# x sent ahead of the powers' row, two transfers moved to GpSimd's queue, guards earlier in a turn: a gated linear attention with a cosine MLP on one core

## The chip, the cores and the metric

The kernel runs on one core of a Trainium2 chip. The metric is device microseconds of that core. The kernel before takes 655.76 us in the median of 3 runs (654.2 to 656.69).

## The reference, cut to what matters

The inputs of the attention have batch 4, 8 heads, 768 steps and 48 channels per head; the MLP takes 3072 rows of 384 channels to 2048 and back. The weights of the MLP arrive as 64-bit floats.

```python
# attention: a gated linear recurrence with complex decay a, |a| capped at 0.999
for t in range(S):
    new_re = ar * S_re - ai * S_im
    new_im = ar * S_im + ai * S_re
    S_re, S_im = new_re + kv, new_im          # kv = outer(k[t], v[t])
    y[:, :, t] = einsum('bhd,bhde->bhe', q[:, :, t], S_re)
# MLP on x = y, with the heads side by side in a row of 384
h = x @ w_in
g = h * cos(h)
out = g @ w_out
```

## The kernel before

The 768 steps of each batch are cut into 6 chunks of 128 steps, and two chunks make a group: 24 chunks and 12 groups (n and g in the code run over them). Within a chunk the recurrence becomes matmuls: running products of the decays (their "powers" P and inverse powers Q) are multiplied into queries and keys, scores sc = k·q are masked into atm, and a state of 96x48 per head carries what came before. A group that begins a batch has no state in its first chunk; one that ends a batch makes no new state after its last chunk. So the groups come in three kinds that recur every three groups.

Groups 0 to 2 are laid out by hand. From group 2 on, a loop runs one turn for each n (line 1568 on), and in it lies work of several groups at once. weave() gives every piece of work a place between 0 and 1: the list chunks(n) spans 0.0 to 0.36, and its entries share that stretch evenly, so an entry's place depends on how many entries the list has. The entries are sorted by place, and a scheduler then settles the order on each engine with that as its priority. Each engine runs its own list in order.

In one turn n there are, by the names of the profile:

- **scores and attention of group n** (chunks): sc and its mask atm, sp (the state sums) and state, then yp, which ScalarE copies to yT. At its end f_x (line 1048) writes yT to DRAM as x, and f_xt (line 1057) reads it back, transposed, as xT.
- **the MLP of group n-1, second half** (products): matmuls into sum and op, and VectorE's ot<-op, which adds an op to a block of the output. out_dram<-ot stores it.
- **the powers of group n+1** (logs, prods): logarithms on ScalarE and VectorE; hi and lo, two halves of the log for exact sums; the matmuls lgs, with hi and lo as right sides; then exponentials into P (tile lg) and Q. When P is done, even_steps sends its last row to DRAM (row_out, line 835) and back, turned, as end (row_back, line 842).
- **phases and keys of group n+1**: phs, then ks and qs, turned by VectorE into tr, sent to DRAM as moved (line 933) and read back as kT (line 936) and qT (line 938).
- **the MLP of group n, first half** (first): 48 float32 matmuls into hp (shown as 96, since a float32 matmul is shown twice), which read xT; sines and products on ScalarE and VectorE.
- **guards** (from n = 4): GpSimd's queue fetches a piece of the 64-bit weights (raw<-in_moe...) once GpSimd has copied one element (after<-gate) to know that a gate is done; VectorE and ScalarE test its exponents. One buffer serves all guards in this part, so a second fetch waits for the first guard's test.

SyncE's queue carries all other transfers of a turn: the loads of re, im, k, q and v, row, x, end, xT, the outputs, moved, kT and qT. An instruction there that waits holds up those behind it. behind() and chain() only fix an order on a queue.

Of the kernel before, what the change touches and what calls it, by code (L numbers as in the profile page):

```python
# [487 lines left out]
def fast_path(ctx, tc, q, k, v, a_re, a_im, moe_w_in, moe_w_out, out, least, odd, wide,  # L488
# [7 lines left out]
    nc = tc.nc  # L496
    B, H, S, D = q.shape
# [45 lines left out]
    def behind(ins, other):  # L543
        tc.add_manual_dep(ins.ins, other.ins.name, mybir.DependencyInfo(
            mybir.DependencyClass.NoSync, mybir.DependencyReason.DATA))
# [21 lines left out]
    def load(g, names, i=None, put=nc.sync.dma_start):  # L567
        for name in names:
            ap = {"re": a_re, "im": a_im, "q": q, "k": k, "v": v}[name]
            if name not in X[g]:  # L570
                X[g][name] = ld.tile([C, G, H, D], F32, tag=name, name=name,
                                     bufs=2 if name == "v" else 1)
            b, c = divmod(g * G + (i or 0), NCH)
            one, n = i or 0, G if i is None else 1
            steps = ap[b].rearrange("h (c p) d -> p c h d", p=C)[:, ds(c, n)]
            tile_ = X[g][name][:, ds(one, n)]
            parts = [(0, C, 0)]
            if name in ("re", "im") and g >= PEG:

                parts = [(0, C - 16, 1), (C - 16, C - 1, 1)]  # L580
                put(out=tile_[C - 1:C], in_=steps[0:1])
            for i_ in range(n):
                for lo, hi, by in parts:
                    put(out=tile_[lo:hi, i_], in_=steps[lo + by:hi + by, i_])
# [227 lines left out]
    def even_steps(g, i, n):  # L812


        x = X[g]
        u = cut(x["mag"], i, n)
        P, Q = cut(x["P"], i, n), cut(x["Q"], i, n)
        ins = [vector.scalar_tensor_tensor(out=u, in0=Q, scalar=HUGE, in1=P,
                                           op0=ALU.min, op1=ALU.mult)]
        yield  # L820
        for t in P, Q:
            ins.append(vector.scalar_tensor_tensor(out=t, in0=u, scalar=3.0, in1=t,
                                                   op0=ALU.subtract, op1=ALU.mult))
            yield

        for one_, what in zip(ins, ("carried", "split")):
            if what in x and g > PEG:
                behind(one_, x[what])
        if g > 0:
            row_out(g, i, n, nc.sync)  # L830
            row_back(g, i, n, nc.sync)

    def row_out(g, i, n, queue):
        P = cut(X[g]["P"], i, n)
        queue.dma_start(out=X[g]["row"][ds(i * DM, n * DM)],
                        in_=P[C - 1:C].rearrange("o x -> (o x)"))

    def row_back(g, i, n, queue):
        row = X[g]["row"][ds(i * DM, n * DM)]
        end = X[g]["end"][:, ds(i * H, n * H)]  # L840
        for a in range(2):
            queue.dma_start(out=end[ds(a * D, D)], in_=row.rearrange("(x d) -> d x", d=D))

    def p_even(g, i, n):
        for _ in even_steps(g, i, n):
# [75 lines left out]
    def f_transpose(g, i, n, name):  # L921


        if i == 0:
            X[g][name] = ft.tile([D2, G * H, Q4, 32] if name == "kT" else [D2, Q4, G * H, 32], F32,
                                 tag=name, name=name, bufs=1)
        tr = ft.tile([C, NB, n * H, 32], F32, tag="tr", name="tr")
        turn = vector.transpose(out=tr, in_=X[g][name[0] + "s"][:, ds(i * H, n * H)].rearrange(
            "p x a d -> p x (a d)").rearrange("p x (r b) -> p b x r", b=NB))
        if name == "qT" and "gated" in X[g - 1]:  # L930
            behind(turn, X[g - 1]["gated"])
        moved = rows_d.tile([Q4, D2, n * H, 32], F32, tag="moved", name="moved", bufs=3)
        nc.sync.dma_start(out=moved.rearrange("q (r b) x j -> (q r) b x j", b=NB), in_=tr)
        if name == "kT":
            for q4 in range(Q4):
                nc.sync.dma_start(out=X[g][name][:, ds(i * H, n * H), q4], in_=moved[q4])
        else:
            nc.sync.dma_start(out=X[g][name][:, :, ds(i * H, n * H)],
                              in_=moved.rearrange("q c x j -> c q x j"))

    def f_turn(g, i, name, hh):

# [109 lines left out]
    def f_xt(g, i=0, n=G):  # L1052

        if i == 0:
            X[g]["xT"] = msb.tile([C, ND, G, C], F32, tag="xT", name="xT")
        moved = X[g]["moved"].rearrange("p s d g t -> (p s d) g t").rearrange("(c r) g t -> r c g t", r=C)
        put = nc.sync.dma_start(out=X[g]["xT"][:, :, ds(i, n)], in_=moved[:, :, ds(i, n)])
        behind(put, late["x"])
        late["x"] = put

    def mm1_sums(g, jp, i=None):

# [97 lines left out]
    def seventh(g, p, part):  # L1160


        x, name = X[g], SEVEN[p]
        if p == 0 and part == 0:
            x["sum"] = pm.tile([C, E2], F32, tag="acc", name="sum", bufs=1)
            x["ot"] = [msb.tile([C, DM], F32, tag="ot", name="ot") for _ in range(G)]

        alone = g == NG - 1 and p == 6
        summed = p in (0, 3, 5, 6) and not alone
        if not summed and part == 0:  # L1170
            x["op"] = pm.tile([C, E2], F32, tag="m", name="op", bufs=2)
        ps = x["sum"] if summed else x["op"]
        for j in range(part * HJ // 2, (part + 1) * HJ // 2):
            matmul(ps, lhsT=left(g, name, j), rhs=right[name][:, j],
                   start=(j == 0 and (p == 0 or not summed)),
                   stop=(j == HJ - 1), skip_group_check=summed)
        if part == 0:
            return
        c11, c12, c21, c22 = (x["ot"][i][:, ts(half, E2)] for i in range(2) for half in range(2))
        if g == NG - 1:  # L1180
            c12 = rest
        if p in (0, 3, 5) or p == 6 and not alone:
            late["scalar"] = scalar.mul(out={0: c11, 3: c21, 5: c22, 6: c12}[p], in_=ps, mul=scale)
        if g == NG - 1 and p == 5:
            scalar.mul(out=c12, in_=ps, mul=scale)
        for part_ in {1: [c11], 2: [c21], 4: [c21, c22], 6: [c12] * alone}.get(p, []):
            added = vector.scalar_tensor_tensor(out=part_, in0=ps, scalar=scale,
                                                in1=part_, op0=ALU.mult, op1=ALU.add)
            if alone:
                behind(added, late["read DVE"])  # L1190
            late["vector"] = added
        row = g * G * C
        if g == NG - 1 and p == 1:
            behind(nc.sync.dma_start(out=out[ds(row, C), 0:E2], in_=c11), late["line"])
        elif p == 4:
            put = nc.sync.dma_start(out=out[ds(row + C, C), :], in_=x["ot"][1])
            if g == NG - 1:
                behind(put, late["read SP"])
        elif p == 6 and alone:
            late["store"] = lambda: nc.scalar.dma_start(out=out[ds(row, C), E2:DM], in_=c12)  # L1200
        elif p == 6:
            nc.sync.dma_start(out=out[ds(row, C), :], in_=x["ot"][0])
# [57 lines left out]
    def chunks(g):  # L1260
        for n in range(g * G, g * G + G):
            for hh in range(2):
                yield lambda n=n, hh=hh: f_scores(n, hh)
            yield lambda n=n: f_state(n)
            yield lambda n=n: f_out(n)
        yield lambda: (f_x(g), f_xt(g))
        if g + 2 < NG:
            yield lambda: load(g + 2, ("k", "q", "v"))

    def first(g):  # L1270
        order = range(NJ // 2) if g < PLAIN else (0, 4, 1, 5, 2, 6, 3, 7)
# [2 lines left out]
    def second(g, i):  # L1274
        return [lambda j0=j0: mm2(g, i, j0, 4) for j0 in range(0, NJ, 4)] if g < PLAIN else []
# [292 lines left out]
    for n in range(2, NG):  # L1568
        weave((mixes(n - 1, 2, 4), 0.0, 0.12), (logs(n + 1), 0.0, 0.02), (chunks(n), 0.0, 0.36),
              (upper[2:] if n == 2 else [], 0.0, 0.2), (products(n - 1, 0, 2 + (n < NG - 1)), 0.0, 0.36),  # L1570
              (prods(n + 1), 0.25, 0.27), (second(n - 1, 1), 0.36, 0.5),
              (products(n - 1, 2 + (n < NG - 1), 7), 0.4, 0.56),
              (phases(n + 1), *((0.472, 0.476) if n == PLAIN else (0.516, 0.524))),
              (keys(n + 1), *((0.5, 0.62) if n == PLAIN else (0.53, 0.64))),
              (last_quarter() if n == PLAIN else [], 0.9, 1.0), (first(n), 0.56, 1.0),
              (mixes(n, 0, 2), 0.9, 1.0), (guarded(n - 1, per) if n > 3 else [], 0.1, 0.9))
    checked = verdict(late, temp)

    def judged():
# [98 lines left out]
```

## Time and profile before

The profiled execution took 653.01 us; its span is 651.2 us, and 1.8 us lie around it.

| what | value |
|---|---|
| median of 3 runs | 655.76 us (654.2 to 656.69) |
| profiled execution, span | 653.01 us, 651.2 us |
| TensorE busy (matmuls), weight loads | 98%, 89% of the span |
| VectorE, ScalarE, GpSimd busy | 76%, 60%, 5% |
| clock granted to TensorE | 1.00 |
| one turn of the loop | 50.2 to 51.7 us, the last 48.1 us |
| SyncE's queue: share of 16 DMA engines | 45.3% |
| GpSimd's queue: share of 16 DMA engines | 11.7% |

A turn is measured here from the first hp matmul of one group to that of the next. The busy share of a matmul row says only that something was in the array; whether the array was delayed is seen from the waits and from the distance between groups of matmuls.

### The profile page before, as it was taken

Reading aid. Unit: us, or ns where it says so; the run is one execution under the profiler, and the core shown is the slowest. Engines: PE = TensorE matmul, PEld = TensorE weight load, DVE = VectorE, ACT = ScalarE, POOL = GpSimd, SP = SyncE. Lnnn points to the kernel's source line nnn. Section 1 sums busy time; section 2 is a strip of 40 time slices with the busy share of each in tenths; the row PEclk is TensorE's granted clock in tenths of the full one; section 3 lists DMA queues with packets and bytes.
Section 4 is the critical chain, followed back from the end, with each engine's and each line's share of the span. In section 5 each row is a group of like instructions: output and inputs, shape, how many; then the busy total and the mean of one; then the engine's idle time right before and its main releaser. Section 6 shows DMA issues by size and latency. Waiting matters only on the chain.

```text
span 651.2 us, 10758 instructions
## 1 busy us (share of the span) xinstructions
PE 641.0 (98%) x4075; PEld 576.4 (89%) x4075; DVE 492.0 (76%) x799; ACT 392.8 (60%) x726; POOL 30.9 (5%) x53
## 2 busy tenths in 40 slices
PE   8999999999999999999999999999999999999997
PEld 6888877777999999899899899899899999999996
DVE  6999989888687688786787787876877878862251
ACT  7898687284583593494494485485576476433330
POOL 4010200000000000010010010000000000000000
PEclk9999999999999999999999999999999999999999
DMA  9968755727627656747738737836836843363001
GB/s 249 244 179 203 225 164 123 170 62 182 146 49 182 158 146 148 194 110 167 209 82 191 204 85 167 205 96 151 226 105 146 219 123 98 112 134 120 25 1 31
DMA packets 232920, 94.90 MB, mean 146 GB/s; under 512 B 208701, under 2 KB 221246, under 8 KB 232858
## 3 DMA queue, kind: packets, MB, share of 16 engines
q1 hardware_dynamic: 225320, 68.51, 45.3%
q0 software_dynamic: 5824, 25.50, 11.7%
q8 instruction: 34, 0.56, 0.4%
q10 hardware_dynamic: 1714, 0.11, 0.2%
q14 instruction: 28, 0.23, 0.1%
HBM read 69.28 MB, written 24.81 MB: 144 GB/s over the span
## 4 chain that ended last, share of the span: by engine, by line
PE 92%; ACT 4%; DVE 3%; DMA 0%; issue 0%; SPq 0%; DVEq 0%
PE hp L687 38%; PE op L687 18%; PE sum L687 16%; PE sc L687 6%; PE yp L687 6%; PE sp L687 4%; PE phs L687 2%; PE lgs L687 1%; ACT tan L707 1%; PE yr L687 1%; PE tp L948 1%; ACT rs L707 1%; ACT lg L707 1%; ACT L703 1%; DVE mag L676 1%; DVE atm L676 1%
## 5 line engine op out<-in xcount | busy, mean ns | idle before, releaser
L687 PE MATMUL hp<-xT,w_in 128*128 128x256 f32 (+1 forms) x1176 | 252.5, 375 | 0.0
L687 PEld LDWEIGHTS hp<-xT,w_in 128*128 128x128 f32 x1176 | 219.6, 190 | 30.2 <-issue 0.2
L707 ACT ACTIVATE gate<-hp,half_pi_b 128x512 f32<-128x512 f32 x96 | 66.0, 687 | 118.5 <-PE hp L687 118.5
L687 PE MATMUL op<-w_out,gate 128*128 128x192 f32 (+1 forms) x448 | 100.7, 374 | 0.0
L676 DVE TENSOR_TENSOR gate<-hp,gate 128x512 f32<-128x512 f32 x96 | 65.7, 684 | 45.8 <-ACT junk L676 45.7
L687 PEld LDWEIGHTS op<-w_out,gate 128*128 128x128 f32 x448 | 75.9, 190 | 16.9 <-issue 2.0
L676 ACT ACTIVATE junk<-hp 128x512 bf16<-128x512 f32 x96 | 56.7, 591 | 0.0
L687 PE MATMUL sum<-t_s,s 128*128 128x192 f32 x320 | 56.3, 329 | 0.0
L687 PEld LDWEIGHTS sum<-t_s,s 128*128 128x128 f32 x320 | 52.1, 190 | 1.5 <-issue 1.5
L676 DVE TENSOR_TENSOR atm<-sc,causal 128x512 f32<-128x512 f32 x48 | 32.9, 689 | 23.4 <-PE sc L687 23.4
L687 PEld LDWEIGHTS sc<-qT,kT 96*128 96x128 f32 x384 | 47.4, 192 | 2.3 <-issue 0.6
L687 PE MATMUL sc<-qT,kT 96*128 96x128 f32 x384 | 49.0, 276 | 0.2 <-ACT qT L676 0.2
L676 ACT ACTIVATE ot<-sum 128x192 f32<-128x192 f32 x39 | 12.6, 322 | 53.7 <-PE sum L687 53.4
L676 DVE SCALAR_TENSOR_TENSOR ot<-op,ot 128x192 f32<-128x192 f32 x40 | 13.3, 354 | 38.0 <-PE op L687 36.4
L687 PE MATMUL yp<-atm,v 128*48 128x128 f32 x352 | 33.6, 277 | 0.9 <-ACT Q L707 0.6
L703 ACT ACT_TABLE_LOAD x24 | 30.8, 1283 | 1.2 <-PEq L1662 0.7
L676 ACT COPY yT<-yp 48x512 f32<-48x512 f32 x44 | 25.3, 574 | 7.4 <-PE yp L687 7.0
L687 PE MATMUL yp<-qT,state 96*48 96x128 f32 x304 | 29.7, 272 | 0.0
L687 PE MATMUL sum<-w_out,gate 128*128 128x192 f32 x160 | 29.7, 329 | 0.0
L687 PE MATMUL sp<-v,ks 128*96 128x48 f32 x320 | 29.7, 245 | 0.0
L687 PEld LDWEIGHTS sp<-v,ks 128*96 128x96 f32 x320 | 29.6, 165 | 0.0
L676 ACT CAST tan<-phs 128x384 int32<-128x384 f32 x24 | 11.4, 480 | 29.4 <-PE phs L687 29.4
(147 smaller groups left out, 987.4 us busy)
## 6 DMA issues: line engine op xcount, KB each, us to landing
moved<-tr SPq DMA_DIRECT2D x20, 768.0 KB
raw<-in_moe_w_in_dram POOLq DMA_DIRECT2D x16, 768.0 KB, 5.1
raw<-in_moe_w_out_dram POOLq DMA_DIRECT2D x16, 768.0 KB, 4.6
kT<-moved SPq DMA_DIRECT2D x40, 192.0 KB
qT<-moved SPq DMA_DIRECT2D x10, 768.0 KB
k<-in_k_dram SPq DMA_DIRECT2D x24, 192.0 KB
q<-in_q_dram SPq DMA_DIRECT2D x24, 192.0 KB
v<-in_v_dram SPq DMA_DIRECT2D x24, 192.0 KB
```

The costliest lines, as they stand in the source:

```text
L676: ins = getattr(self.engine, op)(**kw)
L687: chain(nc.tensor.matmul(out, **kw), "tensor")
L703: chain(nc.scalar.preload_act_table_set(table))
L707: chain(nc.scalar.activation(func=func, **kw))
L948: chain(nc.tensor.transpose(ps[:, h], X[g][name[0] + "s"][:, x0 + h].rearrange("p a d -> p (a d)"), ident), "tensor")
```

## The change

- On SyncE's queue, for groups after the second, P's row is no longer sent when P is done, but in a step of its own, ends(n+1), woven in at 0.36 to 0.37, after x (and ordered behind it). end follows.
- The load of k, q and v two groups ahead, which was the last entry of chunks(n), goes into ends(n+1), each DMA ordered behind end. chunks(n) has 9 entries instead of 10.
- xT, from group 2 on, and qT, from group 3 on, are issued from GpSimd's queue, where they stand in one fixed order with the guards' fetches.
- One store of the output (p == 4) is ordered behind end and the loads.
- The guards are woven in at 0.0 to 0.38 of a turn, not 0.1 to 0.9.

```diff
@@ even_steps
-        if g > 0:
-            row_out(g, i, n, nc.sync)
-            row_back(g, i, n, nc.sync)
+        if 0 < g <= PLAIN:
+            ends(g)
+
+    def after_ends(**kw):
+        put = nc.sync.dma_start(**kw)
+        behind(put, late["ends"])
+        late["ends"] = put
+
+    def ends(g):
+        put = row_out(g, 0, G, nc.sync)
+        if g > PLAIN:
+            behind(put, late["x"])
+        row_back(g, 0, G, nc.sync)
+        if PLAIN < g < NG - 1:
+            load(g + 1, ("k", "q", "v"), put=after_ends)
@@ row_back
-            queue.dma_start(out=end[ds(a * D, D)], in_=row.rearrange("(x d) -> d x", d=D))
+            late["ends"] = queue.dma_start(out=end[ds(a * D, D)], in_=row.rearrange("(x d) -> d x", d=D))
@@ f_transpose
-            nc.sync.dma_start(out=X[g][name][:, :, ds(i * H, n * H)],
-                              in_=moved.rearrange("q c x j -> c q x j"))
+            queue = nc.sync if g <= PLAIN else nc.gpsimd
+            put = queue.dma_start(out=X[g][name][:, :, ds(i * H, n * H)],
+                                  in_=moved.rearrange("q c x j -> c q x j"))
+            if g > PLAIN:
+                chain(put, "gpsimd")
@@ f_xt
-        put = nc.sync.dma_start(out=X[g]["xT"][:, :, ds(i, n)], in_=moved[:, :, ds(i, n)])
-        behind(put, late["x"])
-        late["x"] = put
+        queue = nc.sync if g < PLAIN else nc.gpsimd
+        put = queue.dma_start(out=X[g]["xT"][:, :, ds(i, n)], in_=moved[:, :, ds(i, n)])
+        if g >= PLAIN:
+            chain(put, "gpsimd")
@@ seventh
-            if g == NG - 1:
-                behind(put, late["read SP"])
+            behind(put, late["read SP"] if g == NG - 1 else late["ends"])
@@ chunks
-        if g + 2 < NG:
-            yield lambda: load(g + 2, ("k", "q", "v"))
@@ the loop of turns
-              (prods(n + 1), 0.25, 0.27), (second(n - 1, 1), 0.36, 0.5),
+              (prods(n + 1), 0.25, 0.27),
+              ([lambda: ends(n + 1)] if n + 1 < NG else [], 0.36, 0.37), (second(n - 1, 1), 0.36, 0.5),
...
-              (mixes(n, 0, 2), 0.9, 1.0), (guarded(n - 1, per) if n > 3 else [], 0.1, 0.9))
+              (mixes(n, 0, 2), 0.9, 1.0), (guarded(n - 1, per) if n > 3 else [], 0.0, 0.38))
```

More of the change, by code (lines that the diff above doesn't have):

```diff
@@ L828, in even_steps @@
                 behind(one_, x[what])
-        if g > 0:
-            row_out(g, i, n, nc.sync)
-            row_back(g, i, n, nc.sync)
+        if 0 < g <= PLAIN:
[11 more added lines that the diff above has]
+            load(g + 1, ("k", "q", "v"), put=after_ends)
     def row_out(g, i, n, queue):
         P = cut(X[g]["P"], i, n)
-        queue.dma_start(out=X[g]["row"][ds(i * DM, n * DM)],
-                        in_=P[C - 1:C].rearrange("o x -> (o x)"))
+        return queue.dma_start(out=X[g]["row"][ds(i * DM, n * DM)],
+                               in_=P[C - 1:C].rearrange("o x -> (o x)"))
     def row_back(g, i, n, queue):
```

## The prediction, written before the changed kernel was run

> **What bounds the kernel now.** I read the page first, then TensorE's waits, then turns as windows, then the chain of waits and the timeline inside a turn. The page gives 98% for TensorE's matmuls; since matmuls overlap, I don't take that as proof. TensorE's waits are the proof (columns: waiting group, releaser, us in total, times, longest):
>
> ```profile
> PE busy L687 <- DVE one_b L557: 1.5, 1, 1.5
> PE phs L687 <- ACT tan L707: 1.4, 2, 0.8
> PE yp L687 <- ACT Q L707: 0.6, 1, 0.6
> PE tp L948 <- DVE ks L676: 0.6, 2, 0.4
> ...
> PE sc L687 <- ACT qT L676: 0.2, 1, 0.2
> ```
>
> Seven rows sum to 5.1 us, and none is a wait for a transfer (the last row is a copy by ScalarE at the start, at 23.5 us); the change hurries transfers. Turns, as windows from hp to hp (start:end, us, then busy us of each engine):
>
> ```profile
> 204.16:255.37 51.21, 51.21 (x349) 47.89 (x347) 40.10 (x65) 31.81 (x60) 1.86 (x3) 1.00 0.62 156
> 255.37:305.61 50.24, 50.09 (x332) 46.46 (x332) 38.65 (x62) 31.80 (x60) 1.85 (x3) 1.00 0.63 155
> 305.61:355.93 50.32, 50.32 (x332) 47.00 (x331) 39.76 (x64) 31.79 (x60) 1.85 (x3) 1.00 0.65 162
> ...
> 507.69:559.38 51.69, 51.54 (x349) 47.93 (x347) 40.40 (x68) 31.77 (x60) 1.78 (x3) 1.00 0.48 129
> ```
>
> The first three are the three kinds of turn, all dense with matmuls. The fourth is of the first's kind (349 matmuls) and 51.69 - 51.21 = 0.48 us longer. It is turn n = 10, where the list of chunks had no load left to append (there is no group 12), so it had 9 entries instead of 10. That is the order the change gives to all turns n = 3 to 10. The kernel before thus holds one specimen of the new order, and the chain of waits shows its price (start, us, what):
>
> ```profile
> 537.82 0.91 PE sc L687 x8
> 538.72 0.02 issue
> 538.75 0.69 DVE atm L676
> 539.44 0.86 DVE mag L676
> 540.30 0.88 DVE lo L676
> 541.18 0.04 issue
> 541.22 0.79 PE lgs L687 x3
> 542.02 1.32 PE sp L687 x16
> ```
>
> The chain leaves TensorE for VectorE: lgs waits for lo. In the other turns that make a state, sp stands ahead of lgs and fills this time.
>
> **What the Trainium skill says.** "TensorE: Matmul & The Clock Gate", its first table: the array may pull weight loads ahead, while VectorE and ScalarE keep strict order. The trace agrees: lgs' weight load sat 0.40 us for lo, and sp behind it didn't overtake. "DMA: Bandwidth & Descriptors", Specifications, puts the first byte at about 1 us for GpSimd's queue and 0.6 us for SyncE's. The packets' records of this trace have 0.9 us (a guard issued at 289.42, first packet 290.33) and 0.6 us (xT issued at 301.52, first packet 302.13). "SBUF — State Buffer", two separate sides, warns that VectorE's two-port modes keep GpSimd from writing descriptors; the guards' fetches here, issued beside VectorE's work, show no such delay, but none sits beside the keys' VectorE work as qT will.
>
> **The change part by part.**
>
> *x first, xT on GpSimd.* In turn n = 5 yT was ready at 294.93 (copy 294.35 + 0.58), but x issued at 298.33, behind P's row at 297.98 (lg done 296.97 + 0.95). xT issued at 301.52; its last packet ended at 304.31. x's own landing was noticed 1.0 us after its last packet (300.54), so xT was usable by about 305.3, and hp's loads began at 305.45. Over the eight turns from hp at 153.84 to 507.69 the last packet ends 1.3 to 2.4 us ahead of hp, a real slack of 0.3 to 1.4 us. The change starts x up to 3.4 us sooner, less 0.3 us for the slower queue. In the profiled execution this gains nothing, as hp never waited. What is late next is matmul work itself.
>
> *qT on GpSimd.* It no longer queues behind the four kT (314.25 to 319.04), so it can start some 1.7 us sooner. Its last packet came 1.1 to 2.5 us before sc. Only in turn n = 10 could it have cost anything: sc took 0.96 instead of 0.89, and hp 20.79 instead of 20.72. Gain 0 to 0.1; I take 0. If descriptors starve, qT has about 1 + 1.7 us in hand.
>
> *Queues passed.* On GpSimd's queue the order in a turn becomes after, guard, guard, xT, qT. The second fetch waited 9.55 us for the first guard's test and left at 289.42, before x can land (about 298), so xT isn't held: 0. On SyncE's queue row and end still go when P is ready (297.9); p_end needed end only at 308.67. The loads keep their place: 0. Of end's packets and the k loads, which compete with xT, fewer now overlap it.
>
> *Guards sooner.* Both tests already run in the first 45% of a turn in the trace (VectorE's raw at 284.86 and 294.75 in the turn 255.37 to 305.61). They hardly move: 0.
>
> *The reordering on TensorE, from the shorter list.* The entries of chunks move from 0.036 to 0.040 apart. That puts the second state sum from place 0.234 to 0.26, behind lgs (prods start at 0.25); it also parts the second chunk's sc by an op (sc op sc instead of sc sc op). In the built program's order turns n = 3 to 10 read: sc, op, sc, lgs, sp, half a sum, yp, half a sum. The matmuls' number is unchanged. Price by kind:
>
> - n = 5, 8 (no second state): before, lgs already waits: 1.35 us from lgs to the next group against 0.87 elsewhere. By groups before: .89+1.30+.90+1.32+1.46+1.90+1.40+1.79+1.16+1.35+1.90+2.71 = 18.08. After, with the specimen's durations: .89+1.30+.90+1.30+1.41+1.90+1.40+.89+1.31+.81+1.20+1.46+1.90+1.41 = 18.08. Change 0.
> - n = 4, 7: become the specimen: 2 x 0.48 = 0.96, of which 0.07 was in hp, so 2 x 0.41 = 0.8.
> - n = 10: 0.
> - n = 3, 6, 9 (no state at first): VectorE's order there also changes, to atm, ot, mag, lo. ot needs the second op complete. From op at 333.21 (n = 6): first state sums 0.09 longer and ahead of yp, so op starts about 333.13, + 1.40 + 0.89 + 1.31 = op complete at 336.73, sc to 337.54, where lgs is due. ot starts 0.2 later than op's end, 336.95; then 0.27 to mag, 0.87 to lo (both step sizes are those of neighbouring starts in the timeline), lo at 338.1 and done 0.95 later: 339.05. hi, on ScalarE, moves too: an ot and a copy of yT now precede it, 336.35 to about 337.0, done 337.85, so mag and lo can't be sooner than 337.2 and 338.1 either. lgs' low half would have been loaded at 337.73; it stalls 1.35 us. Before there was no stall there (0.87). 3 x 1.35 = 4.05.
>
> ```profile
> 336.35 0.83 ACT L728 ACTIVATE hi<-lg 128x768 fp32r<-128x768 f32 x1
> 337.20 0.95 DVE L676 TENSOR_TENSOR mag<-mag,tan 128x768 f32<-128x768 f32 x1
> 338.07 0.95 DVE L676 SCALAR_TENSOR_TENSOR lo<-lg,hi 128x768 fp32r<-128x768 f32 x1
> 339.81 0.35 DVE L676 SCALAR_TENSOR_TENSOR ot<-op,ot 128x192 f32<-128x192 f32 x1
> ```
>
> Before, ot came after lo, as the last row shows, and sp hid what was left.
>
> Sum in the profiled execution: 0.8 + 4.05 = +4.9 us, 653.0 to 657.9. Bounds: if ot and hi cost no more than in the specimen, 5 x 0.41 = +2.1; if the later yp (1.5 us, for half a sum stands before it) and a ScalarE order with yT behind hi make x late as well, up to 0.5 a turn, +4 more.
>
> **From the profiled execution to the median.** The three runs took 1.2 to 3.7 us more than the profiled one, 2.75 at the median. The trace doesn't show where. Slack of 0.3 us for xT makes late transfers a fair suspect, and those the change would cure: between 0 and all 2.75. I take half. 655.76 + 4.9 - 1.3 = 659.4.
>
> **Rivals.**
>
> - *Only the specimen's price* (+2.1): lgs stalls 0.4 in five turns, since ot turns out not to gate lo. For it: one measured specimen. Against: VectorE's order, and hi. 655.76 + 2.1 - 1.3 = 656.6.
> - *Not slower: the runs' surplus is xT late at hp.* One mechanism: at the eight hp starts with 0.3 to 1.4 us of slack, ordinary scatter of the DMAs costs 2.75 / 8 = 0.34 us each, and x's early start removes it all. It decides once the surplus removed exceeds the stalls added; with the rival above's +2.1 it gives 655.76 - 2.75 + 2.1 = 655.1, with no stalls 653.0. For it: slack under jitter. Against: no wait for xT in any turn traced.
> - *GpSimd's queue holds xT or qT.* A guard's test delayed behind other ScalarE work keeps the second fetch, and so xT, back. ScalarE's test would have to slip by over 8 us; then each microsecond beyond costs 8 turns x 1 us: 665 and more.
>
> **How the numbers follow.** Forecast 0.5, specimen's price 0.22, not slower 0.18, GpSimd's queue 0.10. The time is 659.4. Its own spread is 658.0 (all the surplus gone) to 660.7 (none). The range takes in the specimen's case and the upper half of the third: 654.5 to 661.5. About 0.5% (3.3 us) is what a measurement tells from no change: slower means over 659.0, faster under 652.5. Faster lies below even a stall-free loop, 653.0: 0.06. Slower: 0.6 of the forecast's 0.5 and the queue's 0.10, plus a little of the others: 0.46. The rest, 0.48, is within 0.5%.
>
> **What would show it.** After should show lgs waiting for lo in eight turns, over 1 us in n = 3, 6, 9 and 0.4 in the others; sp right behind lgs; x issued ahead of row; xT and qT on GpSimd's queue with 2 us or more in hand. No lgs waits, or hp beginning late, would prove me wrong; so would turns of 50.3 us throughout.

## The result, and the profile after

The changed kernel takes 660.63 us in the median of 6 runs (659.78 to 661.47), beside 655.07 us for the kernel before on the same chip (6 runs, 653.68 to 656.69). The ratio is 1.0083, with a 95% interval of 1.0068 to 1.0098: slower by 5.6 us. Its profiled execution took 660.9 us, with a span of 659.0 us; the one before had 653.01 and 651.2.

TensorE's waits after the change (columns as before: waiting group, releaser, us in total, times, longest). Groups that also waited before are left out, and two rows of 0.2 us:

```profile
PE lgs L687 <- DVE lo L676: 3.0, 5, 0.9
...
PE hp L687 <- DMA xT<-x: 0.9, 1, 0.9
PE sc L687 <- DMA kT<-moved: 0.8, 1, 0.8
```

The first row is the stall that the prediction describes. The other two are waits for transfers, which the profile before did not have at all. The page still gives 98% busy to TensorE's matmuls, as before: the busy share hides all three.

What the change was meant to do for xT, it does: for groups 2 to 9, xT's last count (the last of the 16 marks by which a transfer reports that it has landed) comes 1.6 to 3.9 us ahead of hp, beside 0.4 to 1.5 us before. As no hp waited for it before, that gains nothing in these two profiles.

Turns of the changed kernel as windows (start:end, us, then busy us of PE, PEld, DVE, ACT, POOL; clock, DMA share, GB/s). They are the turns n = 3, 4, 5, 6, 10 and 11:

```profile
154.14:206.86 52.72, 50.98 (x332) 47.15 (x331) 38.96 (x62) 29.88 (x56) 1.45 (x2) 1.00 0.63 138
206.86:258.42 51.56, 51.41 (x347) 48.05 (x347) 40.27 (x65) 31.85 (x60) 3.32 (x5) 1.00 0.61 153
258.42:308.60 50.18, 50.03 (x333) 46.68 (x331) 38.66 (x62) 31.76 (x60) 3.12 (x5) 1.00 0.64 157
308.60:360.25 51.65, 50.75 (x331) 47.25 (x331) 39.84 (x64) 31.87 (x60) 3.31 (x5) 1.00 0.62 154
...
514.04:565.73 51.69, 51.54 (x349) 47.96 (x347) 40.31 (x68) 31.86 (x60) 3.24 (x5) 1.00 0.44 121
565.73:614.83 49.10, 48.24 (x322) 44.71 (x321) 25.17 (x44) 16.41 (x38) 3.24 (x5) 1.00 0.43 121
```

Turn n = 6 (308.60) now takes 51.65 us where its kind took 50.32, with no more matmul work in it: PE is busy for 50.75 us and idle for 0.90. Turn n = 10, the specimen, is unchanged to the hundredth. Turns n = 3 and n = 11 are longer than their kinds for another reason, which comes below.

The chain of waits inside turn n = 6 (start, us, what):

```profile
337.70 0.89 PE sc L687 x8
338.59 1.32 PE op L687 x8
339.91 0.02 issue
339.93 0.36 DVE ot L676
340.29 0.86 DVE mag L676
341.15 0.88 DVE lo L676
342.03 0.04 issue
342.08 0.80 PE lgs L687 x3
342.88 1.32 PE sp L687 x16
```

The chain leaves TensorE when op ends, goes through three operations of VectorE, ot, mag and lo, and comes back with lgs; sp, which filled this stretch before, stands behind lgs and cannot overtake it.

All turns, in us from hp to hp, with the difference that the prediction gave (its 1.35, 0.41 and 0) beside the one measured between the two profiled executions:

| turn n | 3 | 4 | 5 | 6 | 7 | 8 | 9 | 10 | 11 | sum |
|---|---|---|---|---|---|---|---|---|---|---|
| before | 50.32 | 51.21 | 50.24 | 50.32 | 51.21 | 50.23 | 50.32 | 51.69 | 48.07 | 453.61 |
| after | 52.72 | 51.56 | 50.18 | 51.65 | 51.57 | 50.58 | 51.64 | 51.69 | 49.10 | 460.69 |
| difference | 2.40 | 0.35 | -0.06 | 1.33 | 0.36 | 0.35 | 1.32 | 0 | 1.03 | 7.08 |
| predicted | 1.35 | 0.41 | 0 | 1.35 | 0.41 | 0 | 1.35 | 0 | 0 | 4.87 |

In n = 3, 1.01 us of the 2.40 lies in the distance from hp to sc (21.73 for 20.72): kT is late. In n = 8, 0.33 of the 0.35 lies there too, and kT's last count came at 432.63, just ahead of sc at 432.87. In n = 11, 1.03 us stands in front of the last hp: xT is late. Without these 2.37 us, 4.71 us are left for the reordering.

Two theories follow. The first is the prediction's: the reordering on TensorE, which comes from the shorter list of chunks, costs the time, and the moved transfers gain or lose little. Its rival: the new places of the transfers (x, xT, qT, row, end, loads) cost it, by holding or crowding one another.

### The profile page after: what moved, and what is told of

It is laid out like the page before. It is cut to its first block, busy times and chain, and to the rows that moved or that the text cites. A ratio compares the mean times of both kernels' runs of the same rounds, so it can differ in the third digit from the quotient of the medians.

```text
span 659.0 us, 10778 instructions
## 1 busy us (share of the span) xinstructions
PE 643.3 (98%) x4075; PEld 577.6 (88%) x4075; DVE 492.4 (75%) x799; ACT 393.2 (60%) x726; POOL 44.9 (7%) x72
## 4 chain that ended last, share of the span: by engine, by line
PE 85%; DMA 4%; ACT 4%; DVE 4%; issue 1%; SPq 1%; DVEq 0%; POOLq 0%
PE hp L687 35%; PE op L687 16%; PE sum L687 15%; PE yp L687 6%; PE sc L687 5%; PE sp L687 4%; PE phs L687 2%; DMA x<-yT 1%; PE lgs L687 1%; DVE mag L676 1%; DMA kT<-moved 1%; DVE lo L676 1%; ACT tan L707 1%; PE yr L687 1%; PE tp L963 1%; DMA moved<-tr 1%
## 5 line engine op out<-in xcount | busy, mean ns | idle before, releaser
L687 PE MATMUL sum<-t_s,s 128*128 128x192 f32 x320 | 57.8, 330 | 0.0
```

Source lines behind the costliest of these rows:

```text
L687: chain(nc.tensor.matmul(out, **kw), "tensor")
```

## The experiments

### The order alone, and the transfers alone

**e2_nine** takes the kernel before, with all its queues, and only makes the list of chunks shorter by moving the load out of it into a part of its own.

```diff
@@ chunks (in the kernel before)
-        if g + 2 < NG:
-            yield lambda: load(g + 2, ("k", "q", "v"))
@@ the loop of turns
+              ([lambda: load(n + 2, ("k", "q", "v"))] if n + 2 < NG else [], 0.35, 0.355),
```

> The kernel before with nothing but the list of chunks shortened to nine entries (the load of k, q, v becomes a part of its own at 0.35); all queues as before. Reordering theory: 655.1 + 4.6 = 659.7 us, ratio 1.007, turns of 51.65, 51.55 and 50.2 us. Queue theory: 655, ratio 1.000, since no transfer moved.

It took 660.51 us (658.64 to 663.3) beside 655.31, ratio 1.0072 (1.0043 to 1.01). TensorE's waits in it:

```profile
PE lgs L687 <- DVE lo L676: 2.8, 4, 0.9
PE hp L687 <- DMA xT<-x: 2.4, 1, 2.4
...
PE sc L687 <- DMA qT<-moved: 0.9, 1, 0.9
```

The lgs row of the changed kernel is there, without any change of queue, and TensorE works through its groups of matmuls in the same order as after the change, from the first to the last. Its turns n = 4 to 7 take 51.56, 50.16, 51.64 and 51.56 us, the same as after the change within 0.02. So the shorter list alone gives a slowdown of the size of the whole: 5.2 us, by the interval 2.8 to 6.6. The late xT here lies ahead of the first of these turns, the late qT in n = 10; how much of them is in the ordinary runs is not known.

**e1_ten** goes the other way: the changed kernel with an empty tenth entry in the list, so that places return to 0.036 apart.

```diff
@@ chunks (in the changed kernel)
         yield lambda: (f_x(g), f_xt(g))
+        if g + 2 < NG:
+            yield lambda: None
```

> The changed kernel with an empty tenth entry in the list of chunks, which brings TensorE's order of before back; all queue moves stay. If the reordering is what costs (4.6 us of the changed kernel's turns by its trace), about 656.0 us, ratio to before 1.001 to 1.002, and lgs stands behind sp without a wait. If the transfers on GpSimd's queue are what costs, it stays near 660, ratio 1.007. If both, the rest above 655 is kT or xT late by about 1 to 2 us.

It took 667.39 us (663.55 to 670.23), ratio 1.0172 (1.0135 to 1.0208): a miss. The order on TensorE was that of before, and lgs no longer waited for lo but in the turns where it did before (0.87 us from lgs to the next group in n = 3, 6 and 9). But other waits had come:

```profile
PE sc L687 <- DMA kT<-moved: 5.8, 5, 2.0
PE hp L687 <- DVE gate L676: 2.6, 6, 0.5
```

GpSimd's queue shows why (timeline; start, us, engine, line, operation, idle before and its releaser):

```profile
249.50 0.76 POOL L1073 DMA_DIRECT2D xT<-x  x1 [19.28 <-DMA x<-yT]
250.25 0.74 POOL L629 DMA_DIRECT2D raw<-in_moe_w_in_dram  x1
```

The entry had moved xT to place 0.306, ahead of the second fetch at 0.317. On a queue with one fixed order the second fetch, which the changed kernel issues in this turn at 240.91, more than 9 us ahead of xT, now had to wait for x to land, and went out beside the loads of k, q and v. The issue of the two moved that follow took 5.35 us (3.15 in the changed kernel), and kT came late. In one stretch of 3.4 us, after its longest wait for kT, the clock granted to TensorE was 0.5 besides. So this kernel differs in two things, and its time alone tells nothing of the order.

**f1_order_of_before** mends that: the empty entry, and the guards at 0.0 to 0.36 so that both stay ahead of xT. The order on TensorE, VectorE and ScalarE is then that of the kernel before, but for a guard's test in two turns and one ot; the queues of SyncE and GpSimd are those of the changed kernel. From e1_ten it differs in the guards' place alone.

```diff
@@ chunks (in the changed kernel)
+        if g + 2 < NG:
+            yield lambda: None
@@ the loop of turns
-              ... (guarded(n - 1, per) if n > 3 else [], 0.0, 0.38))
+              ... (guarded(n - 1, per) if n > 3 else [], 0.0, 0.36))
```

> The changed kernel with an empty tenth entry in the list of chunks and the guards ending at 0.36 instead of 0.38. In the earlier run with the tenth entry alone the second guard's fetch slipped behind xT on GpSimd's queue and into the loads of k, q and v; here it stays ahead, so TensorE, VectorE and ScalarE have the order of before, and SyncE's and GpSimd's queues that of the changed kernel. If the reordering alone makes the change slow, and the second fetch made the earlier run slow: 655 to 656.5 us, ratio 1.000 to 1.002, no wait of lgs but in the two turns without a second state and in that of n = 10. If the moved transfers cost in this order too: 660 or more with waits for kT.

It took 655.7 us (22 runs, 654.21 to 660.33) beside 655.52, ratio 1.0013 (1.0 to 1.0026). All the new places of the transfers together cost 0 to 1.7 us. With e2_nine this settles the main question: the reordering is the slowdown. Its runs scatter more, though: five of the 22 took over 657.5 us, and none of the 27 of the kernel before, whose highest is 657.14. The 12 us from e1_ten to this kernel are the price of the wrong place of the guards. One wait for a transfer was left in its profile:

```profile
PE sc L687 <- DMA kT<-moved: 1.7, 1, 1.7
```

### What holds lo

The prediction named two holds on lo in n = 3, 6 and 9: VectorE's ot in front of it, and ScalarE's hi (and what mag needs) behind a copy of yT. **f4_ot_behind_lo** removes the first: in the changed kernel ot is ordered behind lo.

```diff
@@ the split into hi and lo
-        return lambda: vector.scalar_tensor_tensor(out=lo, ...)
+        def lower():
+            late["lo"] = vector.scalar_tensor_tensor(out=lo, ...)
+            return late["lo"]
+        return lower
@@ seventh, where op is added to ot
+            if p == 1 and "lo" in late:
+                behind(added, late["lo"])
```

> The changed kernel with one ot<-op per turn ordered behind lo on VectorE, which moves it only in n = 3, 6 and 9. If ot alone holds lo there, lgs' wait falls from 1.35 to 0.4 us in three turns: 657.8 us. If ScalarE's hi and exponential, moved behind a copy of yT, hold it as well (as the prediction had it), lgs still waits over 1 us and the time is 660 to 660.6.

It took 660.9 us (660.14 to 662.69), ratio 1.0083 (1.0064 to 1.0101): no gain. From lgs to the next group are 1.76 to 1.82 us in n = 3, 6 and 9 instead of 1.96; in its profile, a longer wait of the last hp for xT (1.7 us for 0.9) takes that gain away again. Its timeline in turn n = 6:

```profile
339.67 0.83 ACT L728 ACTIVATE hi<-lg 128x768 fp32r<-128x768 f32 x1
339.80 0.96 DVE L676 TENSOR_TENSOR mag<-mag,tan 128x768 f32<-128x768 f32 x1 [0.63 <-ACT tan L707]
...
340.67 0.95 DVE L676 SCALAR_TENSOR_TENSOR lo<-lg,hi 128x768 fp32r<-128x768 f32 x1
...
341.68 0.19 PEld L687 LDWEIGHTS lgs<-lo,exact 128*128 128x128 f32 x1 [0.94 <-DVE lo L676]
...
342.41 0.35 DVE L676 SCALAR_TENSOR_TENSOR ot<-op,ot 128x192 f32<-128x192 f32 x1
```

ot is gone from in front of lo, and VectorE now idles 0.63 us in its place, for ScalarE's tan. ot held lo for 0.2 us a turn; behind it the work of ScalarE holds lo for the rest. Both holds lie side by side, so that taking one away gains little. That the copy of yT is what makes ScalarE late was not tried by itself. The stall is there because TensorE reaches lgs before its operand is ready; the sp that filled this time before (1.3 us) stands behind it.

### One transfer at a time

**e3_q_sp** puts qT back on SyncE, **e4_x_sp** puts xT back there right behind x, and **f5_order_of_before_q_sp** is f1_order_of_before with qT on SyncE.

```diff
@@ e3_q_sp and f5_order_of_before_q_sp: f_transpose
-            queue = nc.sync if g <= PLAIN else nc.gpsimd
+            queue = nc.sync
@@ e4_x_sp: f_xt
-        queue = nc.sync if g < PLAIN else nc.gpsimd
+        queue = nc.sync
...
+        behind(put, late["x"])
+        late["x"] = put
```

> The changed kernel with qT back on SyncE's queue behind kT. If qT beside kT makes kT late (1.0 us in the turn of group 2 and 0.4 in that of group 7 in the trace), 659.2 us, and kT's last packet ends 4 us or more before sc again. If qT is harmless there, 660.6.

> The changed kernel with xT back on SyncE's queue, right behind x and ahead of P's row. If GpSimd's queue delays xT (1.0 us at the last hp[...]), 659.6 us; if the late xT of the last turn was chance of one execution, 660.6. A cost of its own is possible: row waits behind xT's wait for x, so end and the loads come up to 2 us later.

> The kernel of f1_order_of_before with qT back on SyncE's queue behind kT. If qT beside kT costs by making kT late, below f1 by 1 us or more, and kT's last packet 4 us ahead of sc; if not, the same as f1 within 1 us.

| kernel | us | ratio (95%) | new waits of TensorE |
|---|---|---|---|
| e3_q_sp | 662.43 (660.49 to 665.55) | 1.0101 (1.0072 to 1.013) | sum for ScalarE's ot 2.0, sc for nothing shown 1.8, sc for qT 1.2 |
| e4_x_sp | 681.68 (674.05 to 683.73) | 1.0374 (1.033 to 1.0419) | sc for kT 10.0, hp for xT 4.3, yp for atm 2.6 |
| f5_order_of_before_q_sp | 661.3 (660.83 to 664.18) | 1.0094 (1.0073 to 1.0115) | yp for atm 2.7, hp for xT 2.0, sum for ot 1.6, sc for qT 0.9 |

All three missed: each took longer than either time that was expected of it. None is clean, for the scheduler also changed the order on VectorE and ScalarE, as the waits for ot and atm show. What qT's queue is worth by itself therefore stays open. One thing can be read in them, in the records of the transfers' packets (the pieces in which a transfer is moved), set on the timeline's clock: with qT on SyncE, behind kT, kT's last packet ends 3.0 to 5.1 us ahead of sc, and 3.9 to 5.3 before the change; with qT on GpSimd, in the changed kernel, it ends 0.5 to 2.3 us ahead. The Trainium skill says in "DMA: Bandwidth & Descriptors", Issuing engines are not separate DMA queues, that transfers run on the same 16 DMA engines and interleave, whichever engine started them. That agrees: qT gained about 1.2 us of lead (from 0.6 to 2.0 us ahead of sc to 1.8 to 3.3), and kT paid for it.

e4_x_sp has a reason of its own besides. In turn n = 3 x was issued at 203.14, xT behind it at 206.26, row only at 206.73 and end at 209.40, 6.3 us after x; in the changed kernel end follows x by 3.0 us in the same turn. xT's wait for x's landing held everything behind it on SyncE, which fits the late kT. The waits are not all of its 26 us: the clock granted to TensorE was 0.5 in five stretches, 20.4 us together, and neither the kernel before nor the changed one has such a stretch inside the loop.

### The kernel before, once more

**f3_before_again** is the kernel before, unchanged, for a second profile.

> The kernel before once more, for a second profile of it. If the runs' 2 us above the first profile are transfers that come late, this execution shows waits for xT, kT or qT of about as much as its time lies above 653.0 us; otherwise the surplus lies elsewhere, with turns of 50.3, 51.2 and 50.2 us.

It took 655.44 us, with a span of 653.7: 2.4 more than the first profiled execution. Its turns agree with the first within 0.2 us, but for one, n = 8: 51.78 for 50.23. At its end TensorE waits for xT, by this row of its waits:

```profile
PE hp L687 <- DMA xT<-x: 1.4, 1, 1.4
```

Another 0.41 us lies ahead of the first turn, where lgs waits 0.9 us for VectorE. So in this one execution more than half of the surplus over the first profile is a late transfer, as the prediction suspected; of the other runs there is no trace.

### The two transfers that the change makes late

f1_order_of_before and the changed kernel both have a late kT in n = 3; the changed kernel also has a late xT in front of the last hp. SyncE's queue in turn n = 3 of the changed kernel (timeline):

```profile
154.93 0.36 SPq L1129 DMA_DIRECT2D out_dram<-ot  x1
155.38 1.06 SPq L854 DMA_DIRECT2D end<-row  x2
...
161.09 1.77 SPq L945 DMA_DIRECT2D moved<-tr  x2
165.83 4.04 SPq L948 DMA_DIRECT2D kT<-moved  x4
```

A store of group 1 stands between row and end and waits for its tile; end, the loads and moved queue behind it. In the other turns the store is ordered behind the loads; this one is issued from another line (mm2), which the change left alone. **g2_store_behind** orders it too, and **g1_store_behind_and_last_turn** also gives the tenth entry to the list of n = 10.

```diff
@@ mm2 (in f1_order_of_before)
-            nc.sync.dma_start(out=out[ts(g * G + i, C), :], in_=ot)
+            put = nc.sync.dma_start(out=out[ts(g * G + i, C), :], in_=ot)
+            if (g, i) == (1, 1):
+                behind(put, late["ends"])
@@ g1_store_behind_and_last_turn also: chunks
-        if g + 2 < NG:
+        if g + 1 < NG:
             yield lambda: None
```

> The kernel f1_order_of_before (the change with the engines' order of before) with one store moved on SyncE's queue: the second store of group 1 no longer stands between row and end of group 3 but behind the loads of k, q and v. If the late kT of that turn (1.7 us of waiting at TensorE in f1's profile) comes from this store, which held end and the loads until its tile was ready at 154.66 us, the wait is gone: 655.7 - 1.7 = 654.0 us, ratio about 0.997, and moved and kT are issued some 3 us sooner. Rival: the loads were held by something else (the buffers of k, q and v, or the two queues' sharing of the transfer engines); then the wait stays and the time is 655.7 us, ratio 1.001.

> As g2_store_behind, and the empty tenth entry also in the last turn of the loop but one, so that its second state sum stands ahead of the logarithms' sum there as in the other turns. That turn took 51.56 us in f1's profile against 51.28 of its kind: by the order theory it gains 0.3 to 0.5 us more: 653.6 us, ratio about 0.9965. If the order of that turn doesn't matter, it is the same as g2_store_behind. Slower than g2_store_behind only if an operation falls later against another engine in that turn, which would show as a new wait of TensorE between 560 and 615 us.

g2_store_behind took 655.26 us (653.66 to 657.71), ratio 0.9995 (0.9983 to 1.0008); g1_store_behind_and_last_turn took 654.1 us (653.4 to 656.16), ratio 0.9978 (0.9966 to 0.9989), both beside 655.48. The same queue in g2_store_behind:

```profile
147.44 0.89 SPq L854 DMA_DIRECT2D end<-row  x2
...
154.80 0.48 SPq L1129 DMA_DIRECT2D out_dram<-ot  x1
159.37 3.34 SPq L945 DMA_DIRECT2D moved<-tr  x2
162.80 4.58 SPq L948 DMA_DIRECT2D kT<-moved  x4
```

kT starts 3 us sooner, and turn n = 3 takes 50.32 us, its time before, instead of f1's 52.22. The cause of the late kT is shown. Yet g2 was expected at 654.0 us and missed, and its profiled execution is no shorter than f1's (spans of 654.0 and 653.7 us), because in both g kernels the last hp waits 1.4 us for xT; in f1 TensorE came there later (609.53 for 609.07) and waited only 0.1 us. In turn n = 10, with the tenth entry, g1 takes 51.21 us for g2's 51.54: the last 0.3 us of the reordering. Its median lies 1.2 us below g2's; the trace accounts for 0.3 of that, and the two intervals overlap.

That last xT is the other late transfer. The timeline of the changed kernel ahead of its last hp (at 614.83):

```profile
600.12 1.18 SPq L1063 DMA_DIRECT2D x<-yT  x2
601.35 0.45 SPq L1634 DMA_DIRECT2D line_d<-low  x1
610.78 0.75 POOL L1073 DMA_DIRECT2D xT<-x  x1 [14.06 <-DMA x<-yT]
```

x's last packet ended at 603.20, and xT, which waits for x's landing, went out 7.6 us later. In eight of the other nine such issues this takes 0.9 to 1.0 us. What is special is line_d<-low, 96 single values of 4 bytes for a verdict on the data's range: the code orders it behind late["x"], which was xT before the change and is x after it. The change had moved it in front of xT without naming it. Two kernels, both from g1, take it away from behind x: **g4_last_x_sp** returns the last group's xT to SyncE between the two, and **g5_line_d_pool** puts line_d behind xT on GpSimd.

```diff
@@ g4_last_x_sp: f_xt
-        queue = nc.sync if g < PLAIN else nc.gpsimd
+        queue = nc.sync if g < PLAIN or g == NG - 1 else nc.gpsimd
...
-        if g >= PLAIN:
+        if g == NG - 1:
+            behind(put, late["x"])
+            late["x"] = put
+        elif g >= PLAIN:
@@ g5_line_d_pool: verdict
-        behind(nc.sync.dma_start(out=line_d[0:D2], ...), late["x"])
-        nc.sync.dma_start(out=line_d[D2:D2 + C], ...)
+        behind(nc.gpsimd.dma_start(out=line_d[0:D2], ...), late["xT"])
+        nc.gpsimd.dma_start(out=line_d[D2:D2 + C], ...)
```

> g1_store_behind_and_last_turn with the last group's xT back on SyncE, behind x and ahead of the small write line_d<-low, as before the change; in that turn no row, end or loads stand behind it. In g1's trace the last xT is issued 8.4 us after x's last packet (1.4 to 1.6 us in eight of the other nine turns), and TensorE waits 1.4 us for it. Theory: line_d<-low, which the change moved directly behind x, delays the landing of x's second half. Then xT is issued about 1 us after x's last packet, the wait is gone, and the time is 654.1 - 1.4 = 652.7 us, ratio about 0.9957. If x itself lands late in the last turn, the wait stays: 654.1 us.

> g1_store_behind_and_last_turn with the last xT left on GpSimd and the small writes line_d put behind it on GpSimd's queue, so that only x stands on SyncE. Theory (line_d<-low directly behind x delays x's landing): xT is issued about 1.5 us after x's last packet, as in the other turns, and the time is 652.7 us, ratio about 0.9957. Rival (GpSimd itself is late in that turn, by what it waits for or fetches): the gap stays near 8 us, TensorE's wait of 1.4 us stays, and the time is that of g1, 654.1 us, while g4_last_x_sp gains.

SyncE's queue in g4_last_x_sp, then GpSimd's in g5_line_d_pool, where x was issued at 593.76:

```profile
595.00 1.46 SPq L1063 DMA_DIRECT2D x<-yT  x2
599.02 0.38 SPq L1073 DMA_DIRECT2D xT<-x  x1
599.45 0.48 SPq L1641 DMA_DIRECT2D line_d<-low  x1
```

```profile
597.81 0.75 POOL L1073 DMA_DIRECT2D xT<-x  x1 [7.31 <-DMA x<-yT]
598.54 0.55 POOL L1639 DMA_DIRECT2D line_d<-low  x1
```

x's last packet ended at 598.61 and 596.89, so xT follows after 0.41 us on SyncE and 0.91 on GpSimd. In both, the last hp no longer waits, and turn n = 11 takes 48.07 us, as before the change. GpSimd itself was not late: the small write directly behind x was the cause.

In time g4_last_x_sp gives 653.97 us (653.32 to 655.04) beside 655.42, ratio 0.9976 (0.9965 to 0.9986), and g5_line_d_pool 655.4 us (654.5 to 655.79), ratio 0.9994 (0.9982 to 1.0006). Both were expected at 652.7, and both missed. g4's equals g1's 0.9978; the profile of either is about 1 us above its own median (655.04 and 655.02), and g4's holds a wait of 1.5 us at 60 to 90 us, in a part that no edit touches. Whether g1's late xT is in its ordinary runs is thus not known. g5 gave its gain back at the end. Its timeline there:

```profile
643.35 0.37 DVE L1646 TENSOR_REDUCE bad<-Q 1x1 f32<-1x224 f32 x1 [4.18 <-DMA Q<-line_d]
...
646.63 0.36 DVE L676 SCALAR_TENSOR_TENSOR rest<-op,rest 128x192 f32<-128x192 f32 x1 [2.05 <-PE op L687]
647.48 2.45 ACTq L1218 DMA_DIRECT2D out_dram<-rest  x1
```

The last store stands behind a branch that reads the verdict. The verdict's first step began 4.9 us before the operation that makes the last result in the kernel before (641.72 and 646.64), and 3.3 us here; the store was issued 0.49 us after that operation's end instead of 0.03, and its issue took 2.45 us instead of 1.17 (1.17 in g1 too). From the last hp to the end of the span are 45.8 us here and 44.5 in g1, which uses up the 1.3 us by which the last hp began sooner (607.44 and 608.73). That g5's median lies 1.3 us above g1's is not explained by the profiles, whose spans are both 653.2 us.

## Why the prediction was right or wrong

*What bounds the kernel, and the specimen.* Right. Turn n = 10 is the same before and after, 51.69 us.

*The reordering on TensorE, +4.9.* Right in mechanism and size. The traces give 4.71 us: 1.39 in n = 3 without the late kT, 1.33 and 1.32 in n = 6 and 9 (1.35 predicted for each), 0.35 and 0.36 in n = 4 and 7 (0.41), -0.06 and 0.02 in n = 5 and 8 (0). e2_nine has it alone at 660.51 - 655.31 = 5.2 us. That both ot and ScalarE's work hold lo, in the step for n = 3, 6 and 9, is shown by f4_ot_behind_lo. Of the signs that the prediction named, the stalls of lgs came as described; hp began late in one turn, n = 11.

*From the profiled execution to the median, -1.3.* Here the sum was off: 3.6 us of slowdown were forecast and 5.6 measured. The suspicion behind the term was sound, for f3_before_again has a late transfer in its surplus. But the term counted only what the change cures. f1_order_of_before measures the moved transfers as a whole at a ratio of 1.0013, that is +0.9 us (0 to 1.7) in place of -1.3. This term makes up the 2 us by which the sum was off. The changed kernel's median lies 0.3 us below its profile, not 1.45 above it.

*Queues passed: 0.* This is the step that failed, and it explains about half of the term above. It followed the moved instructions through one turn in the middle of the loop, and took that turn for all. In n = 3 a store from another line comes between row and end, and the loads don't keep their place behind them: kT is late by 0.8 us in the changed kernel's profile and 1.7 in f1's. In n = 11 line_d passes xT: 0.9 us, and 1.4 in g1 and g2. With the store put right and the order of before, g2_store_behind takes what the kernel before takes (0.9983 to 1.0008), by the ratios 1.2 us less than f1. So the gain of 1.3 us that the prediction counted on did not show even then. g1's 1.4 us contain the better order of n = 10, 0.5 us by the trace (51.21 for 51.69).

*qT on GpSimd: 0.* Its first packet came 1.4 to 1.9 us after its issue, beside 1.4 to 1.5 for the guards' fetches, so missing descriptors cost it 0.5 us at most, and it has more in hand than before. That kT lost some 3 us of its own lead was not seen; in most turns this costs nothing. In n = 3 and 8 of the changed kernel, where kT was late, its part was not measured apart.

*Guards sooner: 0.* Right for the change as it stands, but the stated reason was too weak. e1_ten shows that the guards' place decides whether the second fetch or xT is first on GpSimd's queue, and that the wrong order costs 1.7%. The rival of GpSimd's queue had the hold the other way round, the fetch holding xT; it did not come true.

*Not slower.* It did not come true: the stalls are there, and no gain of the transfers outweighs them. How much of the old surplus was cured, and how much the new late transfers took back, was not measured apart.

*Packet times.* The prediction's packet times stand 0.55 us too early beside the issue times of the timeline. On one clock, the guard's first packet began at 290.89, 1.5 us after its issue, and xT's at 302.69, 1.2 us after: the trace does not confirm the 1 and 0.6 us quoted there. The difference of 0.3 us between the queues holds, and so does xT's slack of 0.3 to 1.4 us, as x's landing was taken from the same records. The expectations of g4_last_x_sp and g5_line_d_pool have the same shift; their 8.4, 1.4 to 1.6 and 1 us are 7.9, 0.9 to 1.0 and 0.4 on one clock.

## What to carry to other kernels

An entry taken out of a list whose places are shared evenly moves all the others: before counting what an edit moves, compare the resulting order on every engine, and look for a matmul that has lost the independent work ahead of it. When a transfer changes queue, follow its old and new neighbours through the first and the last turn too, and everything that was ordered behind it by name, since such an order silently attaches to another instruction. A gain and a loss of one edit are best taken apart by restoring one order while keeping the other, as f1_order_of_before did: of the 0.8% that the change cost, the moved transfers were 0 to 0.3%, and nothing measurable once one store was put right. A transfer that comes sooner saves time only where something waited for it.

## What the runs showed of the hardware

A write of 96 values of 4 bytes to DRAM, line_d<-low, took 7.2 to 9.6 us from its issue to its last count in all fourteen traces, wherever it stood. x goes to DRAM as two writes of 192 KB. In the eight traces where line_d was issued 0.6 to 1.0 us after the second of them, on the same queue, that write's last count came 5.7 to 7.5 us after its last packet, and 0.2 to 0.8 us ahead of line_d's own last count; xT was issued 6.2 to 8.1 us after the last packet. In the other six traces line_d was issued after x had landed. There the last count came 0.3 us after the last packet, and xT's issue after 0.4 us on SyncE and 0.9 on GpSimd. The first of the two writes landed 2.5 us after its issue in all fourteen.

In the kernel before line_d stood directly behind xT, which writes to SBUF, and xT landed without delay: its last count came at 600.69, 0.3 us after its last packet, and line_d's at 605.53. The Trainium skill says in "DMA: Bandwidth & Descriptors", Queues, rings and completion order, that a transfer's count on each DMA engine lands only after every earlier write of that engine. This fits a large write whose count is held by the small write's, if the small one's data were under way first. In the changed kernel the packets of both ended together, x's at 603.20 and those of 4 bytes at 603.25, but the records don't tell which count waited for which. No run here separates the small write's size, its target, its queue and its time. The mechanism stays open; the cost and its cause in the order are shown.
